# Two attention and two gated-ReLU layers on one core: x loaded by block, layernorm statistics of two blocks on VectorE, q and k projected in fours, logit sums and first output projection placed later

## The chip, the cores and the metric

The kernel runs on one core of one Trainium2 chip. The metric is the device time of one launch in microseconds. The engines are TensorE (PE in the profile; its weight loads are PEld), VectorE (DVE), ScalarE (ACT), GpSimd (POOL) and SyncE (SP), which here only issues DMAs. Each engine works through its own instructions in program order, and an instruction that waits holds up what stands behind it on its engine.

## What is computed

Four residual layers over x of 2048 rows and 1024 columns in bfloat16, an attention layer (A) and a gated layer (B), twice, with the same weights:

```python
x = x + A(layernorm(x)); x = x + B(layernorm(x))
x = x + A(layernorm(x)); x = x + B(layernorm(x))

def A(x):                                   # H = 32 heads of 32, W = 8, dil = 2
    q, k, v = heads(x @ wqkv)
    idx = pos[:, None] - 2 * arange(8)      # each row sees itself and 7 rows before it
    logits = where(idx >= 0, einsum("bhsd,bhswd->bhsw", q, k[idx]) / sqrt(32), -1e9)
    return rows(einsum("bhsw,bhswd->bhsd", softmax(logits), v[idx])) @ wo

def B(x):                                   # F = 3584
    gate = x @ W_gate
    return (gate * (gate > 0) * (x @ W_up)) @ W_down
```

## The kernel before

**Tiling.** x stays on the chip as 16 tiles of 128 rows; 4 tiles make a block of 512 rows, and there are 4 blocks (0 to 3) and 4 layers (L = 0 to 3). Every product is made of chunks of 8 matmuls 128x512 that add up in one of 8 PSUM banks. For a block and an attention layer there are 24 chunks of q, k and v (`plan_proj`, L375), the attention on VectorE (`plan_attn`), and 8 chunks of wo (`plan_wo`, L681), whose results VectorE adds to x (L688). A gated layer has 56 chunks for gate and up (L711) and 56 chunks' worth for down (L757).

**The order of work is written by a planner.** `Plan` keeps a planned clock. `on_pe` places a piece of TensorE work right behind the last one, at 0.216 us per matmul; `at(t, f)` places f at planned time t; `on_dve` and `chain` fill VectorE's planned time: the chain is the attention work in order, each piece with a planned duration and a planned time before which it may not start, and the `on_dve` pieces are put in wherever their time has come. At the end all pieces are sorted by planned time and their instructions are issued in that order, each to its own engine. So planned times set only the order on each engine; the real times come from the waits.

**The start (L = 0, block 0).** `First` normalizes block 0 tile by tile, with transposes on TensorE (L334), between the first chunks of v. SP issues, in this order, x tile 0, v's first weights and x tiles 1 to 3, then q's weights in two halves of 1 MB, k's in two halves (L825), the four tiles of block 1's x (L809), and v's second weights (a slab, L202). Then TensorE does q and k of block 0: two chunks of each, then one of q and one of k in turn, and v's second half.

**The logits of block 0** are made in another way than those of all later blocks (`first_logits`). ScalarE copies each q and k chunk out of PSUM (L449, L452). For each chunk c VectorE multiplies q with the 8 shifted k (`mul`, L471, one instruction) and adds that to a float32 sum in two halves (`add`, L481, from c = 1 on, not for the last c). ScalarE then copies the sum to bfloat16 (`split`, L490), VectorE subtracts the copy and the rest is copied again (`rest`, L503), so that three bfloat16 terms, together with the product of the last chunk, stand for the whole sum. TensorE adds them over the partitions with a matrix of ones (`red`, L512, 32 matmuls). `step` puts `red` behind chunk ("v", 0, 1) of the next block's projection. Then come the softmax (`soft_a` L575 to L581, `expo` L584, `soft_b` L589 to L594), the products with v (`pv_mul` L602, `pv_add` L610 to L613) in 8 groups, the stores to `o_d`, and the loads of `oT` (L621) that wo of block 0 needs. That wo stands behind chunk ("k", 0, 1) of block 3's projection (`wo_hook`).

**Layernorm of the later blocks (`plan_ln`).** For each tile ScalarE makes the sum and the sum of squares (`stats`, L225 and L226); for each pair of tiles VectorE does a few operations on 128x2 numbers (`small_a`), GpSimd raises to the power -0.5 (L239, `pow`), VectorE makes the bias (`small_b`, L244), ScalarE normalizes both tiles (`norm`, L250), and SP transposes the pair by DMA into xnT (`turn`, L256). `late_ln(L, b, t, lag)` places this at planned time t, with `lag` ahead of the transposes. For block b + 1 of layer 0 it is placed 9 us after the start of block b's projection.

**Buffers that matter here.** There is one `xn_all` for all layernorms. `term_1` and `term_2` lie in the buffers of k and q (`hm_pool`), so the loads of the next block's q and k (L537) wait until `red` has read them. `ring` holds 5 slabs of weights of 1 MB; k's weights of layer 0 take two of them.

Of the kernel before, what the change touches and what calls it, by code (L numbers as in the profile page):

```python
# [9 lines left out]
BF16 = mybir.dt.bfloat16  # L10
F32 = mybir.dt.float32
ALU = mybir.AluOpType
ACT = mybir.ActivationFunctionType

P = 128
D = 1024
# [5 lines left out]
KC = D // P  # L22
BLK = 512
TPB = BLK // P
EPS = 1e-5
# [19 lines left out]
def _dram(t, off, dims):  # L45
    return bass.AP(tensor=t.tensor, offset=t.offset + off, ap=[list(d) for d in dims])
# [77 lines left out]
def kernel(  # L124
# [11 lines left out]
    nc = tc.nc  # L136
# [3 lines left out]
    NB = S // BLK  # L140
    NT = S // P
# [3 lines left out]
    x_dram = A_x.flatten_outer_dims()  # L145
# [8 lines left out]
    xpool = ctx.enter_context(tc.tile_pool(name="xres", bufs=1))  # L154
    dram = ctx.enter_context(tc.tile_pool(name="dram", bufs=1, space=bass.MemoryType.DRAM))
    wring = ctx.enter_context(tc.tile_pool(name="wring", bufs=1))
    tpose = ctx.enter_context(tc.tile_pool(name="tpose", bufs=4))
    ln_pool = ctx.enter_context(tc.tile_pool(name="ln", bufs=1))
    stat_pool = ctx.enter_context(tc.tile_pool(name="stat", bufs=2))
# [7 lines left out]
    neg_half = const.tile([P, TPB], F32, name="neg_half")  # L167
# [5 lines left out]
    k_d = [dram.tile([D, ROW], BF16, name=f"k_d{b}") for b in range(NB)]  # L173
    v_d = [dram.tile([D, ROW], BF16, name=f"v_d{b}") for b in range(NB)]
    o_d = [dram.tile([TPB, H, DH, P], BF16, name=f"o_d{b}") for b in range(NB)]
    x_tiles = [xpool.tile([P, D], BF16, name=f"x{t}") for t in range(NT)]

    def consts_early():
        nc.gpsimd.memset(ident[:], 1.0)
# [27 lines left out]
    plan = Plan(RING)  # L207
# [1 line left out]
    w0 = {}  # L209


    def plan_ln(L, b, lag=0.5):
        hold = {}
        clock = [0.0]

        def stats(t):
            def f():
                if t == 0:
                    hold["xn"] = ln_pool.tile([P, TPB, D], BF16, tag="xn_all", name="xn_all")
                    hold["T"] = tpose.tile([P, TPB, KC, P], BF16, tag="T", name=f"xnT_{L}_{b}")  # L220
                if t % 2 == 0:
                    hold[("st", t // 2)] = stat_pool.tile([P, 2, 2], F32, tag="st", name=f"st_{L}_{b}")
                st, xt = hold[("st", t // 2)], x_tiles[b * TPB + t]
                junk = hold["xn"][:, t, :]
                nc.scalar.activation(junk, xt[:], ACT.Identity, accum_out=st[:, 0, t % 2:t % 2 + 1])  # L225
                nc.scalar.activation(junk, xt[:], ACT.Square, accum_out=st[:, 1, t % 2:t % 2 + 1])  # L226
            return f

        def small_a(p):
            st = hold[("st", p)]  # L230
            mean = stat_pool.tile([P, 2], F32, tag="mean", name="mean")
            nc.vector.tensor_scalar(mean[:], st[:, 0, :], 1.0 / D, None, op0=ALU.mult)
            nvar = stat_pool.tile([P, 2], F32, tag="nvar", name="nvar")
            nc.vector.tensor_tensor(nvar[:], st[:, 0, :], mean[:], op=ALU.mult)
            nc.vector.tensor_tensor(nvar[:], nvar[:], st[:, 1, :], op=ALU.subtract)
            vpe = stat_pool.tile([P, 2], F32, tag="vpe", name="vpe")
            nc.vector.tensor_scalar(vpe[:], nvar[:], -1.0 / D, EPS, op0=ALU.mult, op1=ALU.add)  # L237
            rstd = stat_pool.tile([P, 2], F32, tag="rstd", name="rstd")
            nc.gpsimd.tensor_tensor(rstd[:], vpe[:], neg_half[:, 0:2], op=ALU.pow)  # L239
            hold[("mean", p)], hold[("rstd", p)] = mean, rstd  # L240

        def small_b(p):
            nb = stat_pool.tile([P, 2], F32, tag="nb", name="nb")
            nc.vector.scalar_tensor_tensor(nb[:], hold[("mean", p)][:], -1.0, hold[("rstd", p)][:], op0=ALU.mult, op1=ALU.mult)  # L244
            hold[("nb", p)] = nb

        def norm(t):
            def f():
                i, rstd, nb = t % 2, hold[("rstd", t // 2)], hold[("nb", t // 2)]
                nc.scalar.activation(hold["xn"][:, t, :], x_tiles[b * TPB + t][:], ACT.Identity,  # L250
                                     scale=rstd[:, i:i + 1], bias=nb[:, i:i + 1])
            return f

        def turn(t):
            def f():
                nc.sync.dma_start_transpose(hold["T"][:, t - 1:t + 1].rearrange("p t k n -> p (t k) n"),  # L256
                                            hold["xn"][:, t - 1:t + 1].rearrange("p t d -> p (t d)"))
                if t == TPB - 1:
                    xnT[(L, b)] = hold["T"]
            return f  # L260

        def row_done(t):
            def f(now):
                e = max(clock[0], now + 0.3)
                plan.at(e, stats(t))
                clock[0] = e + 2.6
                if t % 2 == 1:
                    plan.on_dve(clock[0], 0.7, lambda: small_a(t // 2), lambda n: after_a(n, t))
            return f

        def after_a(now, t):
            plan.on_dve(now + 1.3, 0.2, lambda: small_b(t // 2), lambda n: after_b(n, t))

        def after_b(now, t):
            e = max(clock[0], now + 0.2)
            plan.at(e, norm(t - 1))
            plan.at(e + 1.25, norm(t))
            clock[0] = e + 2.5
            plan.at(clock[0] + lag, turn(t))

        return [row_done(t) for t in range(TPB)]


    class First:
# [12 lines left out]
        def bn(self, t, h):  # L297
            if h == 0:
                self.st[t] = stat_pool.tile([P, 2, 6], F32, tag="bst", name="bst")
            nc.vector.bn_stats(self.st[t][:, h, :], x_tiles[t][:, 512 * h:512 * h + 512])  # L300
# [38 lines left out]
        def begin(self):  # L339
            self.warm(42)  # L340
            self.bn(0, 0), self.bn(0, 1), self.small(0)
            self.norm(0), self.turn(0), self.warm(4)
            self.copy(0, 0)
            self.bn(1, 0), self.bn(1, 1), self.small(1)
            self.copy(0, 1)
            xnT[(0, 0)] = self.T
            self.norm(1), self.bn(2, 0), self.bn(2, 1)
# [12 lines left out]
    def plan_proj(L, b, hooks={}):  # L360
        ends = {}
        hold = {}
# [36 lines left out]
        steps = [(nm, g, j) for nm, g in (("q", 0), ("k", 0), ("q", 1), ("k", 1), ("v", 0), ("v", 1)) for j in range(4)]  # L399
        if first:  # L400

            fst = First()
            plan.at(-1.0, fst.begin)
            w = w0[("v", 0)]
            for t in range(TPB - 1):
                for h, j in ((h, j) for h in range(2) for j in range(4)):
                    plan.on_pe(1, mms("v", 0, j, w, t, t + 1, KC // 2 * h, KC // 2 * (h + 1)), [w])
                    if h == 1 and j == 2:  # L410
                        e = plan.on_pe(2, lambda t=t: fst.turn(t + 1))
                        plan.at(e, lambda t=t: fst.copies(t + 1))
            steps = [("v", 0, j) for j in range(4)] + [("q", 0, 0), ("q", 0, 1), ("k", 0, 0), ("k", 0, 1)]
            steps += [(nm, c // 4, c % 4) for c in range(2, KC) for nm in "qk"] + [("v", 1, j) for j in range(4)]
        for nm, g, j in steps:
            if L == 0:
                w = w0[(nm, g)]
# [3 lines left out]
            if first and (nm, g) == ("v", 0):  # L421
                e = plan.on_pe(2, mms(nm, g, j, w, TPB - 1, TPB), [w])
            else:
                e = plan.on_pe(8, mms(nm, g, j, w), [w])
# [12 lines left out]
    def first_logits(st, tm):  # L437
        hold = {}
# [84 lines left out]
            plan.at(e + T_EV, out)  # L523
            tm["logits_in"] = e + T_EV + 1.5

        return {"evict": evict}, {("v", 0, 1): step}


    def plan_attn(L, b, ends, st, tm):
# [257 lines left out]
    attn = {}  # L787
    glu = {}
    later_hooks = []
    wo_hook = {("k", 0, 1): lambda: wo(0, 0)}  # L790

    def proj(L, b):
        st, tm = {}, {}
        if L == 0 and b == 0:
            hooks, later_hooks[:] = (lambda h: (h[0], [h[1]]))(first_logits(st, tm))
        else:
            hooks = later_hooks.pop() if later_hooks else wo_hook if L == 0 and b == NB - 1 else {}
        attn[(L, b)] = plan_attn(L, b, plan_proj(L, b, hooks), st, tm)

    def wo(L, b):  # L800
        plan_wo(L, b, attn[(L, b)], plan_ln(L + 1, b))

    def late_ln(L, b, t, lag=0.5):
        for i, f in enumerate(plan_ln(L, b, lag)):
            f(t + 2.7 * i)


    def load_x(t, eng=nc.sync):
        return lambda: eng.dma_start(x_tiles[t][:], x_dram[t * P:(t + 1) * P, :])  # L809
# [20 lines left out]
    w0[("v", 1)] = slab(wqkv_v[:, :, 2 * D + SLAB:3 * D], "wv_0_1", -3.0)  # L830
    for t, at in ((1, -6.7), (2, -6.3), (3, -6.2)):
        plan.at(at, load_x(t))
    plan.at(9.0, consts_late)
    for b in range(1, NB):
        for t in range(b * TPB, (b + 1) * TPB):
            plan.at(-4.5 if b == 1 else 41.5 * (b - 1) + 1.0 * (t % TPB), load_x(t))

    for b in range(NB):
        if b + 1 < NB:
            late_ln(0, b + 1, plan.pe + 9.0, 0.5 if b == 0 else 8.0)  # L840
        proj(0, b)
    for b in range(NB):
        if b >= 1:
# [53 lines left out]
```

## Time and profile before

| | |
|---|---|
| median of 3 runs | 1630.63 us (1629.82 to 1632.91) |
| profiled execution | 1630.63 us, its span 1628.8 us |
| mean granted TensorE clock | 0.998 |
| chain that ended last | PE 94%, DVE 2%, DMA 1%, ACT 1%, issue 1% |
| `L711` gate and up | 3584 matmuls, 379 ns each |
| VectorE and ScalarE over the span | 65% and 29% busy |

The page gives the busy time of each engine, then the chain of work that ended last, followed back from the last instruction, and then groups of equal instructions with their duration and with the idle time of their engine before them. Matmuls overlap: one takes 379 ns, but the next starts 216 ns after it, so a run of them is best measured from start to start. A row of the timeline has the start, the length, the engine, the line, the operation with the tile it writes and those it reads, the shapes, how many like instructions were merged, and in square brackets how long the engine was idle before and what ended that.

### The profile page before, as it was taken

The page shows a single profiled execution, that of the slowest core. Times are in us where ns is not written, and L with a number is a line of the kernel's source. Part 1 is how long each engine was busy: PE and PEld are TensorE (multiplying, and loading weights), DVE is VectorE, ACT ScalarE, POOL GpSimd, SP SyncE. Part 2 cuts the span into 40 slices and gives each one's busy share as a digit, 9 for nine tenths or more (in the row PEclk, how much of TensorE's full clock was granted, in tenths as well). Part 3 has the DMA queues.
Part 4 walks back from the last instruction along what each step waited for, and adds up shares of the span by engine and source line. Part 5 has one row for each costly group of instructions (what it writes and reads, how often), then busy time and mean ns, then how long its engine had stood idle before and what let it go on. Part 6 is the DMA issues. An engine that isn't in the chain of part 4 may idle for free.

```text
span 1628.8 us, 19258 instructions
## 1 busy us (share of the span) xinstructions
PE 1615.7 (99%) x7658; PEld 746.9 (46%) x7658; DVE 1051.0 (65%) x1272; ACT 466.6 (29%) x739; POOL 114.8 (7%) x172
## 2 busy tenths in 40 slices
PE   9989999999999999999999999999999999999999
PEld 7434444444444444444444444444444444444444
DVE  4979989989999259880599716996989211211211
ACT  5665511304230341303413151133021301221110
POOL 3212000001000100011000110000000000000000
PEclk9999999999999999999999999999999999999999
DMA  7678678777956979568886699599846655565442
GB/s 235 166 181 171 187 184 216 195 205 200 237 163 194 257 191 232 160 212 231 198 215 184 199 238 208 160 279 240 220 150 198 197 169 162 175 176 161 156 163 70
DMA packets 443883, 314.83 MB, mean 193 GB/s; under 512 B 195696, under 2 KB 437776, under 8 KB 443792
## 3 DMA queue, kind: packets, MB, share of 16 engines
q1 hardware_dynamic: 414624, 281.39, 64.8%
q10 hardware_dynamic: 24368, 23.40, 4.5%
q0 software_dynamic: 4800, 8.80, 1.6%
q8 instruction: 60, 0.98, 0.3%
q14 instruction: 31, 0.25, 0.1%
HBM read 261.77 MB, written 36.05 MB: 183 GB/s over the span
## 4 chain that ended last, share of the span: by engine, by line
PE 94%; DVE 2%; DMA 1%; ACT 1%; issue 1%; SPq 0%; POOL 0%; ACTq 0%; DVEq 0%
PE acc_u L711 24%; PE acc_g L711 24%; PE dacc L757 24%; PE acc_wo L681 7%; PE acc_v L375 5%; PE acc_q L375 5%; PE acc_k L375 5%; DVE lacc L481 1%; DMA x<-in_A_x_dram 1%; DVE prod L471 1%; DMA xnT<-xn_all 0%; SPq L825 0%; POOL rstd L239 0%; ACT xn_all L225 0%; ACT term L490 0%
## 5 line engine op out<-in xcount | busy, mean ns | idle before, releaser
L711 PEld LDWEIGHTS <-ring 128*128 128x128 bf16 x3584 | 350.7, 98 | 422.9
L711 PE MATMUL acc_g<-xnT,ring 128*128 128x512 bf16 x1792 | 423.3, 379 | 0.0
L711 PE MATMUL acc_u<-xnT,ring 128*128 128x512 bf16 x1792 | 423.3, 379 | 0.0
L757 PE MATMUL dacc<-ring,hT 128*128 128x512 bf16 (+1 forms) x1820 | 388.1, 376 | 0.0
L726 DVE TENSOR_TENSOR hT<-acc_u,r 128x512 bf16<-128x512 f32 x224 | 154.2, 689 | 324.2 <-PE acc_u L711 318.1
L718 ACT ACTIVATE r<-acc_g 128x512 bf16<-128x512 f32 x224 | 133.6, 596 | 709.9 <-PE acc_g L711 709.9
L757 PEld LDWEIGHTS <-hT 128*128 128x128 bf16 x1820 | 178.1, 98 | 209.0
L375 PEld LDWEIGHTS <-ring 128*128 128x128 bf16 x1152 | 115.6, 100 | 133.0
L602 DVE TENSOR_TENSOR pvt<-a,vhm 128x4096 bf16<-128x4096 bf16 x64 | 146.2, 2284 | 0.2
L561 DVE TENSOR_TENSOR l<-l,pr 128x1024 f32<-128x1024 f32 x112 | 136.7, 1221 | 2.2
L551 DVE TENSOR_TENSOR pr<-qhm,khm 128x4096 bf16<-128x4096 bf16 x56 | 127.8, 2282 | 14.2 <-DMA khm<-k_d 14.2
L765 DVE TENSOR_TENSOR x<-dacc,x 128x512 bf16<-128x512 f32 (+1 forms) x65 | 42.8, 679 | 125.4 <-PE dacc L757 125.2
L375 PE MATMUL acc_k<-xnT,ring 128*128 128x512 bf16 x512 | 114.1, 379 | 0.0
L681 PE MATMUL acc_wo<-ring,oT 128*128 128x512 bf16 x512 | 111.8, 379 | 0.0
L375 PE MATMUL acc_v<-xnT,ring 128*128 128x512 bf16 x384 | 84.2, 379 | 0.0
L225 ACT ACTIVATE xn_all<-x 128x1024 bf16<-128x1024 bf16 x60 | 63.3, 1054 | 68.0 <-DVE x L688 62.7
L613 POOL DMA_DIRECT2D o_d<-ohm x64 | 35.4, 553 | 619.9 <-DVE ohm L612 602.8
L610 DVE TENSOR_TENSOR pvt<-pvt 128x2048 bf16<-128x2048 bf16 x64 | 78.1, 1220 | 1.2
L250 ACT ACTIVATE xn_all<-x,nb,rstd 128x1024 bf16<-128x1024 bf16 x60 | 72.2, 1234 | 19.9 <-DVE nb L244 16.3
L681 PEld LDWEIGHTS <-oT 128*128 128x128 bf16 x512 | 50.2, 98 | 60.4
L384 ACT CAST stage_q<-acc_q 128x512 bf16<-128x512 f32 x56 | 32.5, 582 | 157.8 <-PE acc_q L375 154.4
L239 POOL TENSOR_TENSOR rstd<-vpe,neg_half 128x2 f32<-128x2 f32 x30 | 37.0, 1235 | 552.9 <-DVE vpe L237 400.8
(80 smaller groups left out, 839.1 us busy)
## 6 DMA issues: line engine op xcount, KB each, us to landing
ring<-in_B_W_gate_dram SPq DMA_DIRECT2D x56, 1024.0 KB, 7.4
ring<-in_B_W_up_dram SPq DMA_DIRECT2D x56, 1024.0 KB, 5.5
ring<-in_B_W_down_dram SPq DMA_DIRECT2D x48, 1024.0 KB, 6.0
ring<-in_A_wqkv_dram SPq DMA_DIRECT2D x27, 1024.0 KB, 5.6
ring<-in_A_wo_dram SPq DMA_DIRECT2D x16, 1024.0 KB, 7.3
vhm<-v_d SPq DMA_DIRECT2D x32, 284.0 KB, 7.4
v_d<-stage_v ACTq DMA_DIRECT2D x32, 256.0 KB, 6.4
o_d<-ohm POOLq DMA_DIRECT2D x64, 128.0 KB, 4.1
```

Of the source, the lines that this page charges most:

```text
L225: nc.scalar.activation(junk, xt[:], ACT.Identity, accum_out=st[:, 0, t % 2:t % 2 + 1])
L250: nc.scalar.activation(hold["xn"][:, t, :], x_tiles[b * TPB + t][:], ACT.Identity, scale=rstd[:, i:i + 1], bias=nb[:, i:i + 1])
L375: nc.tensor.matmul(acc[:, t0 * P:t1 * P], lhsT=lhsT, rhs=xnT[(L, b)][:, t0:t1, kc, :], start=(kc == 0), stop=(kc == KC - 1))
L551: nc.vector.tensor_tensor(pr[:], st["q"][:], _ap(st["k"], HALO - DIL * w, [[HALO + P, DH], [1, P]]), op=ALU.mult)
L561: nc.vector.tensor_tensor(l[:], pr[:, 0:8] if i == 0 else l[:], pr[:, 8 * i + 8:8 * i + 16], op=ALU.add)
L602: nc.vector.tensor_tensor(tt[:], a_bc, v_sh, op=ALU.mult)
L610: nc.vector.tensor_tensor(tt[:, 0:4], tt[:, 0:4], tt[:, 4:8], op=ALU.add)
L681: nc.tensor.matmul(acc[:], lhsT=st["oT"][:, c, t, :], rhs=ws[half]["t"][:, c, :], start=(c == 0), stop=(c == KC - 1))
L711: nc.tensor.matmul(acc[:], lhsT=w["t"][:, kc, (j % 4) * P:(j % 4 + 1) * P], rhs=xnT[(L, b)][:, :, kc, :], start=(kc == 0), stop=(kc == KC ...
L718: nc.scalar.activation(r[:], hold.pop(("g", j))[:], ACT.Relu)
L726: nc.vector.tensor_tensor(st["hT"][:, j, :], hold.pop(("u", j))[:], hold.pop(("r", j))[:], op=ALU.mult)
L757: nc.tensor.matmul(accs[(t, c0)][:], lhsT=st["hT"][:, j, t * P:(t + 1) * P], rhs=w["t"][:, jl, c0 - half * SLAB:c0 - half * SLAB + n], sta ...
```

## The change

- Blocks 1 to 3 of x become one tile of four (`x_blk`). Block 1 is loaded by one DMA ahead of k's weights, block 2 by one DMA behind v's second slab, block 3 by two at planned time 45; before, each tile had its own load, block 1's behind k's weights, the others at planned times 41.5 and 83 and after.
- For blocks 1 and 3 VectorE takes the statistics (`bn_stats`, two for each tile, and `bn_aggr`) in place of ScalarE; block 2 stays on ScalarE. The three layernorms are placed at 9, 37 and 75.5, the norms of block 3 not before 87, and the transposes' lag is 0.5 for all.
- Block 0's projection goes in fours: v, q, k, q, k, v.
- `red` stands behind ("v", 1, 0) and wo of block 0 behind ("k", 0, 2).
- The constants of GpSimd (`consts_late`) are placed at 22 in place of 9.

```diff
+    x_blk = [xpool.tile([P, TPB, D], BF16, name=f"xb{b}") if b else None for b in range(NB)]
+    x_tiles = [x_blk[t // TPB][:, t % TPB, :] if t >= TPB else xpool.tile([P, D], BF16, name=f"x{t}") for t in range(NT)]
-    x_tiles = [xpool.tile([P, D], BF16, name=f"x{t}") for t in range(NT)]
...
-    def plan_ln(L, b, lag=0.5):
+    def plan_ln(L, b, lag=0.5, on_vector=False, norm_at=0.0):
...
+        def bn(t):
+            def f():
+                if t == 0:
+                    begin()
+                if t % 2 == 0:
+                    hold[("bn", t // 2)] = stat_pool.tile([P, 2, 2, 6], F32, tag="bst2", name="bst2")
+                for h in range(2):
+                    nc.vector.bn_stats(hold[("bn", t // 2)][:, t % 2, h, :], x_tiles[b * TPB + t][:, 512 * h:512 * h + 512])
+            return f
...
         def small_a(p):
+            if on_vector:
+                mv = stat_pool.tile([P, 2, 2], F32, tag="mv2", name="mv2")
+                for i in range(2):
+                    nc.vector.bn_aggr(mv[:, i, :], hold[("bn", p)][:, i].rearrange("p a b -> p (a b)"))
+                nc.vector.tensor_scalar(vpe[:], mv[:, :, 1], EPS, None, op0=ALU.add)
+                nc.gpsimd.tensor_tensor(rstd[:], vpe[:], neg_half[:, 0:2], op=ALU.pow)
+                hold[("mean", p)], hold[("rstd", p)] = mv[:, :, 0], rstd
+                return
...
                 e = max(clock[0], now + 0.3)
-                plan.at(e, stats(t))
-                clock[0] = e + 2.6
+                if on_vector:
+                    plan.on_dve(e, 1.4, bn(t))
+                    clock[0] = e + 1.4
+                else:
+                    plan.at(e, stats(t))
+                    clock[0] = e + 2.6
...
-            e = max(clock[0], now + 0.2)
+            e = max(clock[0], now + 0.2, norm_at)
             plan.at(e, norm(t - 1))
...
-            steps = [("v", 0, j) for j in range(4)] + [("q", 0, 0), ("q", 0, 1), ("k", 0, 0), ("k", 0, 1)]
-            steps += [(nm, c // 4, c % 4) for c in range(2, KC) for nm in "qk"] + [("v", 1, j) for j in range(4)]
+            steps = [(nm, g, j) for nm, g in (("v", 0), ("q", 0), ("k", 0), ("q", 1), ("k", 1), ("v", 1)) for j in range(4)]
...
-        return {"evict": evict}, {("v", 0, 1): step}
+        return {"evict": evict}, {("v", 1, 0): step}
...
-    wo_hook = {("k", 0, 1): lambda: wo(0, 0)}
+    wo_hook = {("k", 0, 2): lambda: wo(0, 0)}
...
-    plan.at(9.0, consts_late)
-    for b in range(1, NB):
-        for t in range(b * TPB, (b + 1) * TPB):
-            plan.at(-4.5 if b == 1 else 41.5 * (b - 1) + 1.0 * (t % TPB), load_x(t))
+    plan.at(22.0, consts_late)
+    for b, n, at in ((1, 4, -5.7), (2, 4, -2.5), (3, 2, 45.0)):
+        for i in range(0, TPB, n):
+            plan.at(at, lambda b=b, n=n, i=i: nc.sync.dma_start(
+                x_blk[b][:, i:i + n, :], _dram(x_dram, (b * BLK + i * P) * D, [[D, P], [P * D, n], [1, D]])))
 
     for b in range(NB):
-        if b + 1 < NB:
-            late_ln(0, b + 1, plan.pe + 9.0, 0.5 if b == 0 else 8.0)
+        if b == 0:
+            late_ln(0, 1, 9.0, on_vector=True)
+            late_ln(0, 2, 37.0)
+            late_ln(0, 3, 75.5, on_vector=True, norm_at=87.0)
         proj(0, b)
```

More of the change, by code (lines that the diff above doesn't have):

```diff
@@ L209, with begin @@
     w0 = {}
-    def plan_ln(L, b, lag=0.5):
+    def plan_ln(L, b, lag=0.5, on_vector=False, norm_at=0.0):
         hold = {}
         clock = [0.0]
+        def begin():
+            hold["xn"] = ln_pool.tile([P, TPB, D], BF16, tag="xn_all", name="xn_all")
+            hold["T"] = tpose.tile([P, TPB, KC, P], BF16, tag="T", name=f"xnT_{L}_{b}")
+        def bn(t):
[7 more added lines that the diff above has]
+            return f
         def stats(t):
@@ L218, in f @@
                 if t == 0:
-                    hold["xn"] = ln_pool.tile([P, TPB, D], BF16, tag="xn_all", name="xn_all")
-                    hold["T"] = tpose.tile([P, TPB, KC, P], BF16, tag="T", name=f"xnT_{L}_{b}")
+                    begin()
                 if t % 2 == 0:
@@ L229, in small_a @@
         def small_a(p):
+            rstd = stat_pool.tile([P, 2], F32, tag="rstd", name="rstd")
+            vpe = stat_pool.tile([P, 2], F32, tag="vpe", name="vpe")
+            if on_vector:
[6 more added lines that the diff above has]
+                return
             st = hold[("st", p)]
@@ L235, in small_a @@
             nc.vector.tensor_tensor(nvar[:], nvar[:], st[:, 1, :], op=ALU.subtract)
-            vpe = stat_pool.tile([P, 2], F32, tag="vpe", name="vpe")
             nc.vector.tensor_scalar(vpe[:], nvar[:], -1.0 / D, EPS, op0=ALU.mult, op1=ALU.add)
-            rstd = stat_pool.tile([P, 2], F32, tag="rstd", name="rstd")
             nc.gpsimd.tensor_tensor(rstd[:], vpe[:], neg_half[:, 0:2], op=ALU.pow)
-            hold[("mean", p)], hold[("rstd", p)] = mean, rstd
+            hold[("mean", p)], hold[("rstd", p)] = mean[:], rstd
         def small_b(p):
             nb = stat_pool.tile([P, 2], F32, tag="nb", name="nb")
-            nc.vector.scalar_tensor_tensor(nb[:], hold[("mean", p)][:], -1.0, hold[("rstd", p)][:], op0=ALU.mult, op1=ALU.mult)
+            nc.vector.scalar_tensor_tensor(nb[:], hold[("mean", p)], -1.0, hold[("rstd", p)][:], op0=ALU.mult, op1=ALU.mult)
             hold[("nb", p)] = nb
@@ L801, in wo, with late_ln @@
         plan_wo(L, b, attn[(L, b)], plan_ln(L + 1, b))
-    def late_ln(L, b, t, lag=0.5):
-        for i, f in enumerate(plan_ln(L, b, lag)):
-            f(t + 2.7 * i)
+    def late_ln(L, b, t, lag=0.5, on_vector=False, norm_at=0.0):
+        for i, f in enumerate(plan_ln(L, b, lag, on_vector, norm_at)):
+            f(t + 2.7 * i * (not on_vector))
     def load_x(t, eng=nc.sync):
```

## The prediction

> **What bounds the kernel now.** I read the page first, then TensorE's waits, its timeline over the first 200 us, VectorE's timeline there, and the landings of the first loads.
>
> ```profile
> PE 1615.7 (99%) x7658; PEld 746.9 (46%) x7658; DVE 1051.0 (65%) x1272; ACT 466.6 (29%) x739; POOL 114.8 (7%) x172
> ```
>
> TensorE (PE) is busy 99%: only what makes it wait can be won. Its waits, longest first, are all in the first 150 us: 4.9 us for the copies of the logit terms (L490), 1.4 at its first instruction, 1.3 for the last term (L503), 1.2 for xnT, and three below 0.5. In its timeline (start, length, engine, line, idle time before and its releaser):
>
> ```profile
> 80.09 3.62 PE L375 MATMUL acc_v<-xnT,wqv 128*128 128x512 bf16 x16
> 83.64 0.61 PE L512 MATMUL L<-prod,wide 128*32 128x512 bf16 x8
> 84.08 0.60 PE L512 MATMUL L<-term,wide 128*32 128x512 bf16 x8
> 84.95 0.40 PE L512 MATMUL L<-term,wide 128*32 128x512 bf16 x4 [0.26 <-ACT term L490]
> 90.03 1.04 PE L512 MATMUL L<-term,wide 128*32 128x512 bf16 x8 [4.68 <-ACT term L490]
> 92.36 0.62 PE L512 MATMUL L<-term,wide 128*32 128x512 bf16 x4 [1.28 <-DVE term L503]
> 92.92 5.07 PE L375 MATMUL acc_v<-xnT,wqv 128*128 128x512 bf16 x16
> 97.82 7.07 PE L375 MATMUL acc_v<-xnT,ring 128*128 128x512 bf16 x32
> 139.26 7.07 PE L375 MATMUL acc_v<-xnT,ring 128*128 128x512 bf16 x32
> 147.51 7.07 PE L375 MATMUL acc_q<-xnT,wqv 128*128 128x512 bf16 x32 [1.18 <-DMA xnT<-xn_all]
> ```
>
> See three losses. The 32 logit sums (L512) need 4 x 0.44 = 1.76 us when nothing waits (8 of them from 83.64 to 84.08) but fill 83.55 to 92.92: **7.61 us**. The 16 matmuls behind them take 4.90 to the next start, where 16 elsewhere take 3.45 (half of 6.91): **1.45**, at a slow array clock. Block 3's xnT comes late: 147.51 - 139.26 - 6.91 = **1.34**. What feeds the sums is VectorE's chain:
>
> ```profile
> 28.08 2.29 DVE L471 TENSOR_TENSOR prod<-q_fm,k_fm 128x4096 bf16<-128x4096 bf16 x1 [12.15 <-ACT k_fm L452]
> 53.32 2.28 DVE L471 TENSOR_TENSOR prod<-q_fm,k_fm 128x4096 bf16<-128x4096 bf16 x1
> 60.05 2.28 DVE L471 TENSOR_TENSOR prod<-q_fm,k_fm 128x4096 bf16<-128x4096 bf16 x1
> 84.93 2.29 DVE L503 TENSOR_TENSOR term<-lacc,term 128x2048 bf16<-128x2048 f32 x1 [1.52 <-ACT term L490]
> 90.02 2.29 DVE L503 TENSOR_TENSOR term<-lacc,term 128x2048 bf16<-128x2048 f32 x1 [2.79 <-ACT term L490]
> ```
>
> It idles 12 us before its first product, because ScalarE sits on block 1's late x (waits: 2.6 us, L225) and evicts k's chunk 0 at 27.41, though TensorE had it at 23.1. Then it runs 6.73 us per chunk and ends at 92.31, with small layernorm operations between and two waits for ScalarE, which has block 2's norms ahead of the term copies.
>
> **The change, part by part.** One chunk (8 matmuls) is 1.727 us. The planner's clock and the trace run together from q's start (planned 8.21, seen 17.93): I add 9.7.
>
> *Loads.* Block 1's x, 1 MB in one issue, goes ahead of k's. Landings from issue:
>
> ```profile
> L825 SPq DMA_DIRECT2D ring<-in_A_wqkv_dram x1: 2745/2745/2745, 6.6 to 6.6; - x1
> DMA to landing us min/median/max: 14.6/14.6/14.6
> L809 SPq DMA_DIRECT2D x<-in_A_x_dram x1: 1147/1147/1147, 13.1 to 13.1; - x1
> DMA to landing us min/median/max: 12.2/12.2/12.2
> ```
>
> k's second half lands at 6.63 + 14.6 = 21.2, the last of block 1's x at 25.3; q's second half landed at 15.8 (4.73 + 11.1), k's first at 18.5 (5.29 + 13.2). So x1 now lands at about 15.8 + 2.7 = 18.5, and k's second half between 23.9 (2.7 us per MB) and 25.3 (same bytes by then as before). With q in fours, k is first wanted at 17.93 + 4 x 1.727 = 24.84, its second half at 25.7. Taken: no wait, margin 0.4; far bound below. Block 2's x issues right behind v's second slab, block 3's after wo's; both are wanted tens of us later. SP has three issues fewer; its next work, block 1's transposes, waits for the norms anyway.
>
> *Statistics of block 1.* Eight bn_stats at 0.65 (a pair takes 1.29) = 5.2 us, two small_a of 0.6, two small_b: 7.3 us from 18.5, done by 25.8, inside VectorE's 12 us of idle. Without that cover the chain starts up to 5.2 later. ScalarE loses 8 x 1.15 = 9.4 us there. It does norm(0), then evicts k0 (TensorE 26.57, plus 0.2) by 27.4: the first product stays near 27.4 (28.08 now), the second follows k1 and two norms at 30.25.
>
> *The chain then.* Chunks at 6.73 put product 4 at 50.4. Block 2's statistics, planned at 37, put their small operations around it: 4 x 0.16 plus 0.75 for POOL's pow, twice, 2.8. Product 7 is at 73.4, the four L503 at 2.25 follow, end **84.8** against 92.31. ScalarE must keep up: from 46.3 to the first term copy (planned 61.4, so 71.1) it has 14 evictions (8.2), 7 store issues (3.2), stats 9.4, norms 4.8: 25.6 in 24.8, so 1 us late at most, by which VectorE may slip 1 or 2.
>
> *Sums later.* After ("v",1,0) instead of ("v",0,1): three chunks, 5.2 us. TensorE is there at 83.55 + 5.18 = 88.73, 4 us after the last term. The 7.61 and the 1.45 go.
>
> *What waits behind.* SP's first load of block 1's q (L537) needs term_2's buffer, so it now waits for sums that end near 90.5 (92.98 now); behind it stand block 3's transposes, ready near 100 only, then khm. No loss.
>
> *Block 3.* Its bn_stats and small_a (6.5 us) fill VectorE from 84.8 to 91.4, before soft_a, which waits for the sums anyway (90.5 plus 1.1 of copies: 91.6; now 94.06). Without that gap soft_a is 6.5 late. Transposes run near 100 to 110, xnT is wanted at 137: the 1.34 goes. Small operations (4.4 us) leave block 0's pv groups.
>
> *wo of block 0, one chunk later*, is reached at 90.5 + 3 + 24 + 7 chunks = 149.2. soft_a 91.6, exp behind one eviction, soft_b (3.8) to 99.6, eight pv groups of 4.66 to 137, then, as now (145.67 to 149.30, landing 3.3 after), oT at 143.9: margin 5.3, now 157.87 - 152.6 = 5.3. Without the later hook it would be 3.6. Later blocks keep their distances to TensorE, within 1 us.
>
> *Constants (L184)* go behind POOL's pows; zpad is wanted at 59.6, wide at 88. Nothing.
>
> **Sum:** 7.61 + 1.45 + 1.34 = 10.4; 1628.8 - 10.4 = 1618.4. The execution took 1630.63, the median, so 1.83 lies around the span: **1620.2**.
>
> **Rivals.**
> A. *The chain is not earlier* (ScalarE's backlog or pow eats the 7.5 us). It ends at 92.3, the sums at 92.98 instead of 90.5: 2.5 us stay, **1622.7**. For: 25.6 us of ScalarE work in 24.8. Against: its two waits today came from norms that now run 15 us earlier. The Trainium skill, "TensorE: Matmul & The Clock Gate", Part 1, has the array at half clock after an idle window of about 3.4 us; the 4.68 us idle here agrees, and by it this shorter wait costs no slow stretch, while without it 1.45 comes on top (1624.2).
> B. *k's weights come last.* If they land at 30.4, as v's slab did (14.30 + 16.1) beside the first v_d stores, TensorE waits 4.7: **1624.9**. Against: the slab had another MB and zpad's small packets beside it.
> C. *ScalarE takes the place of VectorE*: term copies late by as much as the sums moved. The 9.06 stays, 1.34 goes: **1629.3**. It would need 9 us of lag, I find 1 or 2.
> D. *Slower: the shared x tile.* Four x tiles of blocks 1 to 3 become one. If waits were kept per tile, each wo addition (L688) would wait for ScalarE's statistics of its neighbour: a stage is 4 x (1.29 + 2.33) + 2.48 of norms = 17.0 against 13.8, 3.15 in each of six stages, 18.9: **1639.1**; from 1.7 a stage on it is a loss. Against: SP loads a slab of ring at 170.15 while wo's matmuls read another part of it; norm(2) writes xn_all at 39.97 while the transposes of its first half, issued 36.93, are under way.
>
> **Numbers.** Forecast 0.73, A 0.11, B 0.05, C 0.05, D 0.06. 0.2% is 3.3 us, what a measurement here can tell. Below 1627.4 lie forecast, A and B: 0.89; C is the same, 0.05; D slower, 0.06. The median runs spread -0.8 to +2.3 us. The forecast's own range is 1619 to 1623; with A and half of B it is 1618.5 to 1625.
>
> **What would show it.** TensorE's list of waits without L512 or xnT; L512's 32 sums within 2 us; the matmuls behind at 3.45 per 16; VectorE's last L503 ending at 84 to 88 and bn_stats in its two gaps; k's first matmul at 24.84 without a wait; wo of block 0 near 149 without one. A wait at the first acc_k shows B, one at acc_wo a late oT, L688 idle for ScalarE shows D. I am wrong if TensorE waits again after 25 us.

## The result, and the profile after

The changed kernel takes 1621.2 us (median of 6 runs, 1620.36 to 1622.18) against 1630.62 us: a ratio of 0.9941, 95% interval 0.9928 to 0.9954. It is faster by 9.4 us, 0.6%. The profiled execution took 1621.7 us, its span is 1620.0 us, 8.8 less than before.

The page's first line, TensorE still at 99%:

```profile
PE 1609.8 (99%) x7609; PEld 745.5 (46%) x7658; DVE 1060.6 (65%) x1284; ACT 450.5 (28%) x707; POOL 111.1 (7%) x172
```

VectorE has 9.6 us more to do and ScalarE 16 less. TensorE's list of waits is now complete in five rows (engine, line, what it waited for, us in total, times, longest):

```profile
PE warm L321 <- POOL neg_half L183: 1.4, 1, 1.4
PE acc_v L401 <- DMA wqv<-in_A_wqkv_dram: 0.9, 1, 0.9
PE tp L360 <- DVE xn_all L355: 0.8, 1, 0.8
PE acc_k L401 <- DMA ring<-in_A_wqkv_dram: 0.6, 1, 0.6
PE acc_v L401 <- ACT xnT L363: 0.5, 2, 0.2
```

Neither the logit sums nor xnT are in it. New is the 0.6 us at the first k matmuls. The same places in TensorE's timeline (line numbers have moved by some 25):

```profile
18.51 7.08 PE L401 MATMUL acc_q<-xnT,wqv 128*128 128x512 bf16 x32
25.43 1.03 PE L401 MATMUL acc_k<-xnT,ring 128*128 128x512 bf16 x4
27.01 6.26 PE L401 MATMUL acc_k<-xnT,ring 128*128 128x512 bf16 x28 [0.56 <-DMA ring<-in_A_wqkv_dram]
...
88.37 1.89 PE L401 MATMUL acc_v<-xnT,ring 128*128 128x512 bf16 x8
90.19 0.61 PE L537 MATMUL L<-prod,wide 128*32 128x512 bf16 x8
90.63 1.47 PE L537 MATMUL L<-term,wide 128*32 128x512 bf16 x24
92.03 5.35 PE L401 MATMUL acc_v<-xnT,ring 128*128 128x512 bf16 x24
97.22 7.07 PE L401 MATMUL acc_q<-xnT,wqv 128*128 128x512 bf16 x32
```

The sums take 92.03 - 88.37 - 1.73 (one chunk) = 1.93 us where they took 9.37, and the 24 matmuls behind them take 5.19, full speed. From 138.66 on block 3's q follows without a gap, and wo of block 0 begins at 150.75 without one. VectorE's chain, and what it does in the gap behind it:

```profile
78.34 4.49 DVE L528 TENSOR_TENSOR lacc<-lacc,term 128x2048 f32<-128x2048 f32 x2
82.74 4.54 DVE L528 TENSOR_TENSOR term<-lacc,term 128x2048 bf16<-128x2048 f32 x2
87.20 2.46 DVE L228 BATCH_NORM_STATS2 bst<-xb 128x6 f32<-128x512 bf16 x4
```

The last term is done at 87.28, with no wait for ScalarE, and block 3's statistics follow at once.

### The profile page after: what moved, and what is told of

The parts are those of the page before. It is cut to its first block, busy times and chain, and to the rows that moved or that the text cites. A ratio compares the mean times of both kernels' runs of the same rounds, so it can differ in the third digit from the quotient of the medians.

```text
span 1620.0 us, 19174 instructions
## 1 busy us (share of the span) xinstructions
PE 1609.8 (99%) x7609; PEld 745.5 (46%) x7658; DVE 1060.6 (65%) x1284; ACT 450.5 (28%) x707; POOL 111.1 (7%) x172
## 4 chain that ended last, share of the span: by engine, by line
PE 98%; DMA 1%; SPq 1%; issue 0%; DVE 0%; DVEq 0%
PE acc_u L736 24%; PE acc_g L736 24%; PE dacc L782 24%; PE acc_k L401 7%; PE acc_wo L706 7%; PE acc_v L401 6%; PE acc_q L401 6%; DMA ring<-in_A_wqkv_dram 1%; SPq L850 0%; PE L L537 0%; SPq L834 0%; SPq L861 0%; DVE xb L790 0%; SPq L854 0%; SPq L838 0%
## 5 line engine op out<-in xcount | busy, mean ns | idle before, releaser
L790 DVE TENSOR_TENSOR xb<-dacc,xb 128x512 bf16<-128x512 f32 (+1 forms) x49 | 32.6, 678 | 120.4 <-PE dacc L782 120.0
L586 DVE TENSOR_TENSOR l<-pr 128x1024 f32<-128x1024 bf16 x56 | 68.2, 1218 | 0.6
L593 DVE TENSOR_TENSOR l<-l 128x512 f32<-128x512 f32 x112 | 62.3, 556 | 3.0
L261 POOL TENSOR_TENSOR rstd<-vpe,neg_half 128x2 f32<-128x2 f32 x26 | 26.7, 1026 | 540.8 <-DVE vpe L260 540.6
```

The costliest lines, as they stand in the source:

```text
L586: nc.vector.tensor_tensor(l[:], pr[:, 0:8] if i == 0 else l[:], pr[:, 8 * i + 8:8 * i + 16], op=ALU.add)
L593: nc.vector.tensor_tensor(l[:, 0:n], l[:, 0:n], l[:, n:2 * n], op=ALU.add)
```

## The experiments

Every kernel was timed beside the kernel before, at least five runs each, on one chip for each group of four; the ratios are to the kernel before on the same chip. The first moves the sums without the rest of the change, the next six undo one part each, the eighth splits a load. "Loss at the sums" is the time between the chunks on either side of the logit sums (L512, or L537 and L538 where lines have moved) less 1.76 us for the sums, as in the prediction. A "slow stretch" is the run of TensorE matmuls behind a wait that takes longer than its full pace of 0.216 us each.

### The sums alone moved

In the kernel before:

```diff
-        return {"evict": evict}, {("v", 0, 1): step}
+        return {"evict": evict}, {("v", 1, 0): step}
-    wo_hook = {("k", 0, 1): lambda: wo(0, 0)}
+    wo_hook = {("q", 1, 1): lambda: wo(0, 0)}
```

> The kernel before with the logit sums behind ("v", 1, 0) and wo of block 0 behind ("k", 0, 3); loads, statistics and the order of q and k as before. My theory: moving the sums alone takes most of their stall away, because VectorE's chain still ends at 92.3 while TensorE now reaches the sums at 88.7, so 2.5 us of 9.06 stay; but block 3's transposes hang on VectorE and ScalarE, which do not move, so xnT still lands near 147, and what is won comes back there as a longer wait (1.3 grows to about 7): 1629 us. Rival, every loss is won by itself: 1624.0 us, with the wait for xnT still near 1.3.

The kernel that ran differs from this text in one place: wo of block 0 stands behind ("q", 1, 1), four chunks later than in the kernel before, and not behind ("k", 0, 3), which would be two.

Measured: 1638.56 us, ratio 1.005 (1.0038 to 1.0063): **slower than before**. Both theories missed, mine in the place and the size. TensorE's timeline of that kernel:

```profile
92.60 5.35 PE L375 MATMUL acc_v<-xnT,ring 128*128 128x512 bf16 x24
103.31 9.18 PE L375 MATMUL acc_q<-xnT,wqv 128*128 128x512 bf16 x32 [5.36 <-DMA xnT<-xn_all]
112.33 7.07 PE L375 MATMUL acc_k<-xnT,ring 128*128 128x512 bf16 x32
...
207.71 3.57 PE L711 MATMUL acc_g<-xnT,ring 128*128 128x512 bf16 x8 [4.38 <-DMA xnT<-xn_all]
```

SP's queue in the same stretch:

```profile
92.71 0.54 SPq L537 DMA_DIRECT2D qhm<-q_d  x1
93.29 4.16 SPq L256 DMA_TRANSPOSE xnT<-xn_all  x1
```

and in the kernel before:

```profile
93.02 0.54 SPq L537 DMA_DIRECT2D qhm<-q_d  x1
93.61 3.90 SPq L256 DMA_TRANSPOSE xnT<-xn_all  x1
```

The loss at the sums fell from 7.61 to 2.08 and the slow stretch behind them (1.45) went, nearly as expected. But block **2**, not 3, now comes late: the second half of its transposes stands on SP behind the load of q (L537), which waits until the sums have read term_2's buffer. Its norms are done at 88.1, and it is issued at 93.29, where TensorE wants its result at 97.8. The kernel before has the same order and nearly the same times, but there TensorE, held up at the sums, wants the result only at 104.73: the stall at the sums hid this wait. It costs 5.53 (103.31 - 92.60 - 5.18), 2.11 of slow matmuls behind it, and 1.04 go at block 3. Gate and up also wait for their xnT, 4.54 and 2.79 of slow matmuls: wo of block 0 begins at 165.18 in place of 157.87, and the last transposes that hang on it are issued at 192.75, behind two 1 MB loads, and land 14.8 us later. In all 18.1 where the kernel before loses 10.4. Without these 7.3 it would be 10.8, so by the trace the sums alone win nothing, and that this kernel is slower comes from wo's place. A kernel with the sums moved and wo less far was not run.

### The changed kernel with one part undone

**Sums back.** `{("v", 1, 0): step}` becomes `{("v", 0, 1): step}`.

> The changed kernel with the logit sums back behind ("v", 0, 1). My theory: the chain itself is 5 us earlier, so TensorE, there at 84.9, waits for a last term that ends at 87.3: a loss of 1.1 us, an idle time too short for a slow stretch behind it, 1622.3 us. Rival, the later place is what removed the stall: 5 us or more stay and the slow stretch comes back, 1626 us or more.

Measured: 1621.51 us, 0.9945 (0.9932 to 0.9959), the same as the changed kernel. One wait of 0.63 us at the sums (loss 1.00), no slow stretch: as my theory has it. Once the chain is early, the later place of the sums adds nothing that can be timed.

**x behind k.** Block 1's load at -5.2 in place of -5.7.

> The changed kernel with block 1's x loaded behind k's weights instead of ahead. My theory: TensorE's 0.6 us wait at the first acc_k goes, k's second half landing near 24.3, but x lands near 27, the statistics end near 33.6, the first product starts some 5 us later, the chain ends near 92 and TensorE waits 1.5 to 2 us at the sums: 1622.2 us. Rival, only k's lateness counts: 1620.5 us, no wait at the sums.

Measured: 1620.67 us, 0.9935 (0.9923 to 0.9948); the rival's number. x landed at 25.4, not 27, the first product started at 32.52, 3.8 us later and not 5, and the chain ended at 89.88, not 92; the other half of the difference is that block 2's small operations waited less for pow (0.61 and 0.59 where the changed kernel waited 1.80 and 0.59). With the sums at 89.30 that is just in time, loss 0.18. So x ahead of k is not needed either, though without it there is no margin left: the last term is ready 0.6 us after the sums begin.

**q and k in turn.** The two lines of `steps` of the kernel before.

> The changed kernel with q and k of block 0 in turn as before. My theory: the fours are there for k's weights: k's second half is then wanted at 22.8 and lands at 27.0, so TensorE waits about 4.1 us instead of 0.6 and all behind it moves: 1624.6 us, or 1626 if a slow stretch follows that wait. Rival, the fours are there for VectorE's chain (wait at the sums) and k's place is harmless: 1621 us with no wait at acc_k beyond 1 us.

Measured: 1626.68 us, 0.9970 (0.9958 to 0.9981), the second of my numbers. The wait is at the place named, with a slow stretch behind it (12 matmuls in 4.34 us, 1.75 too many):

```profile
21.09 1.07 PE L401 MATMUL acc_k<-xnT,ring 128*128 128x512 bf16 x4
26.74 4.50 PE L401 MATMUL acc_k<-xnT,ring 128*128 128x512 bf16 x12 [4.58 <-DMA ring<-in_A_wqkv_dram]
31.08 1.89 PE L401 MATMUL acc_q<-xnT,wqv 128*128 128x512 bf16 x8
```

**Block 1's statistics on ScalarE.** `late_ln(0, 1, 9.0)`.

> The changed kernel with block 1's statistics on ScalarE as before (x still loaded ahead of k). My theory: 9.4 us of statistics on ScalarE between 19 and 31 hold up the copy of k's chunk 0, the first product starts near 31.7 instead of 28.75, 2.8 us of small operations go into the chain, which ends near 93: TensorE waits about 2 us at the sums, 1623.3 us. Rival, VectorE's statistics of block 1 buy nothing, the early x and the later sums are enough: 1621.2 us, no wait at the sums.

Measured: 1620.76 us, 0.9935 (0.9922 to 0.9947); the rival's number. The first product started at 29.30, not 31.7, and the chain ended at 88.19, not 93: a loss of 0.17 at the sums. I had laid all four tiles' statistics, 9.4 us, ahead of k's first copy; in the trace three of them stand ahead of it (it starts at 28.68) and the fourth behind it.

**wo of block 0 back.** `("k", 0, 1)`, and `t + 4.0` for `t + 5.0` in `after_pv`.

> The changed kernel with wo of block 0 back behind ("k", 0, 1), two instead of three k chunks ahead of it being done; the planned time of oT's loads is put 1 us earlier, so that they still stand ahead of it in the order. My theory: oT lands at 144.9 and wo would begin at 149.0, margin 4: no wait, 1621.2 us. Rival, wo's later place is needed to hide oT: a wait at acc_wo of 1 us or more and 1622.5 us or more.

Measured: 1621.13 us, 0.9938 (0.9924 to 0.9952), no wait at acc_wo: my theory. With oT's loads planned 1 us earlier, wo's later place is not needed.

**Block 3's statistics on ScalarE.** `late_ln(0, 3, 75.5, norm_at=87.0)`.

> The changed kernel with block 3's statistics on ScalarE as before, at the same planned times. My theory: VectorE's gap before soft_a is free, so what stands in it costs and saves nothing; ScalarE's 9.4 us delay the copies of the sums and with them soft_a by a few us, which the 5.8 us ahead of wo of block 0 take up: 1621.2 us, no wait at acc_wo or xnT. Rival, VectorE's statistics of block 3 are needed: oT or xnT comes late, TensorE waits 1 us or more.

Measured: 1620.63 us, 0.9935 (0.9922 to 0.9947): my theory. TensorE's only wait past the start is 1.3 us for k's weights. The price is paid in margin: oT's first load is issued at 146.05 and lands 3.1 later, 1.8 us ahead of wo where the changed kernel has 5.8.

**x in two halves around k.**

```diff
-    for b, n, at in ((1, 4, -5.7), (2, 4, -2.5), (3, 2, 45.0)):
+    for b, n, at in ((1, 2, -5.7), (2, 4, -2.5), (3, 2, 45.0)):
...
-            plan.at(at, lambda b=b, n=n, i=i: nc.sync.dma_start(
+            plan.at(at + 0.5 * (b == 1 and i > 0), lambda b=b, n=n, i=i: nc.sync.dma_start(
```

> The changed kernel with block 1's x in two loads of two tiles, one ahead of k's weights and one behind them. My theory: k's second half lands 1.3 us earlier, at 25.6 against a need at 26.3, so the 0.6 us wait goes; VectorE's statistics of the second pair end some 2 us later, the chain ends near 89.5, still before the sums need it: 1620.5 us. Rival, the chain loses more than that and TensorE waits at the sums: 1621.5 us or more.

Measured: 1620.6 us, 0.9933 (0.9921 to 0.9946). The wait for k is gone and the sums wait for nothing, as my theory has it; the chain ends at 86.9, earlier than the 89.5 it gave. But 0.6 us less than the changed kernel is inside the spread of the runs. It is a version as good as the changed one; that it beats it is not shown.

### What carries the gain

Five of the undone parts cost nothing that can be timed, so the gain has to hang on what they share: the layernorms' places, or any one of several parts that stand in for each other. Four kernels more.

**Only the places.** The changed kernel with all of the above undone: only the layernorms of blocks 2 and 3 stay at 37 and 75.5, with the early loads.

In the changed kernel:

```diff
-            late_ln(0, 1, 9.0, on_vector=True)
+            late_ln(0, 1, 9.0)
             late_ln(0, 2, 37.0)
-            late_ln(0, 3, 75.5, on_vector=True, norm_at=87.0)
+            late_ln(0, 3, 75.5, norm_at=87.0)
```

Besides, x of block 1 at -5.2, q and k in turn, the sums behind ("v", 0, 1), wo behind ("k", 0, 1) and `consts_late` at 9.0.

> Of the change only the earlier places of the layernorms of blocks 2 and 3 and the earlier loads of their x: statistics all on ScalarE, block 1's x behind k, q and k in turn, the sums behind ("v", 0, 1), wo of block 0 behind ("k", 0, 1), GpSimd's constants at 9. My theory: with block 2's norms gone from ScalarE's queue ahead of the term copies the chain ends near 88, so some 3.3 us of the 9.06 at the sums stay, without a slow stretch, and the 1.34 at xnT goes: 1623.5 us. Rival, the sums' later place or VectorE's statistics carry the gain: the stall at the sums stays above 6 us, 1627 us or more.

Measured: 1629.01 us, 0.9981 (0.9972 to 0.9990). The 1.34 at block 3's xnT went, as my theory says; the sums did not follow it (a loss of 7.40, and 1.42 behind them), and the number is the rival's:

```profile
84.56 0.62 PE L538 MATMUL L<-term,wide 128*32 128x512 bf16 x8
87.28 0.40 PE L538 MATMUL L<-term,wide 128*32 128x512 bf16 x4 [2.11 <-ACT term L516]
90.11 1.04 PE L538 MATMUL L<-term,wide 128*32 128x512 bf16 x8 [2.42 <-ACT term L516]
92.43 0.62 PE L538 MATMUL L<-term,wide 128*32 128x512 bf16 x4 [1.29 <-DVE term L529]
92.99 5.03 PE L401 MATMUL acc_v<-xnT,wqv 128*128 128x512 bf16 x16
```

The norms no longer hold up the term copies (block 2's last norm ends at 75.3, the first term copy waits for the chain until 78.60). But x of block 1 is now one load and lands as a whole: ScalarE takes its first tile at 25.90, where it took it at 21.98, and the first product starts at 31.99 where it started at 28.08. The chain ends at 92.38, as before. So this kernel also carries a cost of the single load; the early places with block 1's x in four loads were not run.

**Block 2's place back.** `late_ln(0, 2, 51.8, 8.0)` in the changed kernel.

> The changed kernel with block 2's layernorm placed as before (51.8, its transposes 8 us behind the norms). My theory: its second transposes stand behind the load of q on SP that waits for the sums, as in the run with the sums alone moved, so xnT of block 2 comes about 5 us after TensorE wants it at 97, a slow stretch of 2 us follows, and ScalarE's term copies come behind the norms again: 1628 us, with the longest wait at acc_q for xnT. Rival, VectorE's chain alone decides: 1622 us, a wait at the sums and none for xnT.

Measured: 1628.91 us, 0.9992 (0.9983 to 1.0001): the gain is gone, all but at most 0.2%. The loss at the sums is 2.48, xnT of block 2 costs 4.43, the slow matmuls behind it 1.47:

```profile
93.33 5.35 PE L401 MATMUL acc_v<-xnT,ring 128*128 128x512 bf16 x24
102.94 8.54 PE L401 MATMUL acc_q<-xnT,wqv 128*128 128x512 bf16 x32 [4.25 <-DMA xnT<-xn_all]
111.32 7.07 PE L401 MATMUL acc_k<-xnT,ring 128*128 128x512 bf16 x32
```

SP's queue there, and the same transposes in the changed kernel, where q's first load is issued at 92.14, behind them:

```profile
93.44 0.54 SPq L562 DMA_DIRECT2D qhm<-q_d  x1
94.03 4.49 SPq L278 DMA_TRANSPOSE xnT<-xn_all  x1
```

```profile
69.48 3.72 SPq L278 DMA_TRANSPOSE xnT<-xn_all  x1
```

Block 2's norms are done at 88.8, but its second transposes are issued at 94.03, right behind q's first load: SP's queue, as with the sums alone. VectorE waits for ScalarE's term copies again, 4.46 and 2.25, and that is the loss at the sums. A kernel that changes SP's order alone was not run; that the 5.9 us at xnT come from it is read from these rows.

**Block 3's place back.** `late_ln(0, 3, 95.3, 8.0)` and wo behind `("k", 0, 3)`.

> The changed kernel with block 3's layernorm placed as before (95.3, on ScalarE, its transposes 8 us behind the norms), and wo of block 0 behind ("k", 0, 3), where its loads still stand ahead of it. My theory: xnT of block 3 lands near 145, where TensorE wants it at 138.7: a wait of about 6 us with a slow stretch of 1.5 to 2 behind it, 1628 to 1629 us. Rival, with the sums' stall gone all that feeds the transposes comes earlier too, and the wait stays near the 1.3 of before: 1622.5 us.

Measured: 1621.96 us, 0.9952 (0.9938 to 0.9967); the rival's number. xnT lands at 138.58, not 145, and TensorE waits 1.10: with the sums' stall gone, all that feeds these transposes comes earlier too (they are issued from 127.98 on, from 136.95 in the kernel before).

**q and k in turn, x behind k.** Both parts undone together.

> The changed kernel with q and k of block 0 in turn and block 1's x behind k's weights. My theory: the fours are needed only because x goes ahead of k; with both undone the 4.6 us wait at acc_k of the run with q and k in turn is gone, the first product starts near 32 to 33, and the sums wait 0 to 1 us: 1621 us. Rival, q and k in turn cost by themselves: 1624 us or more.

Measured: 1621.25 us, 0.9939 (0.9926 to 0.9951): my theory, with 1.2 us of wait at the sums. So the fours buy nothing that can be timed but room for x ahead of k, and x ahead of k is not needed.

## Why the prediction was right, point by point

- **The three losses** (10.4 us). The sums' 7.61 came to 7.44, because the 32 sums take 1.93 us in place, not 1.76; the slow stretch (1.45) and block 3's xnT (1.34) went entirely. That they are what the kernel had to win holds.
- **k's weights: the term that was mis-sized.** "Taken: no wait, margin 0.4." k's second half landed at 27.0 (issued at 10.0, 17.0 later), not at 25.3, and cost 0.72 us. This is the prediction's own sign of being wrong, a wait of TensorE after 25 us, and the only one. It was to come in at the latest when the same bytes had come in before; the landing was later than that. The price changes from run to run: TensorE's list has none in the kernel with the sums back and 1.3 with block 3 on ScalarE, where the loads stand in the same order and k's second half landed at 25.6 and 27.2. The first half of rival B is thus true, at a seventh of its price.
- **The start.** q of block 0 begins 0.58 us later (18.51 for 17.93). TensorE waited 0.9 us for the second half of v's first weights, which the change does not touch; they landed at about 9.1 (2.74 + 6.4), and at about 8.5 (2.74 + 5.8) before. Kernels whose start is the same as the changed one's begin q at 18.00 (sums back) and 18.72 (wo back), so the runs scatter here by as much. With 0.17, 0.72 and 0.58 off, 10.4 becomes 8.9; the spans differ by 8.8. The median's 9.4 is larger, as the six spans run from 1618.7 to 1620.5 and the profiled one is among the slow half.
- **The chain.** Forecast to end at 84.8 with a slip of 1 or 2, it ended at 87.28: 1.3 of that is the later start (28.75 for 27.4), 1.2 one longer wait for pow (1.80 for 0.6). That wait is GpSimd's queue and not pow itself, which took 0.72 there: ahead of it stood a store of v, issued at 57.41, that waited for ScalarE's copy. ScalarE was not late for it at all: it waited 1.94 for the chain before its first copy. The forecast of 25.6 us of work in 24.8 was too dark. (In it 8 x 1.15 is 9.2 and not 9.4; the statistics' rows start 1.18 apart, which gives the 9.4.)
- **What waits behind.** SP's load of q waits for the sums (issued at 92.14), block 3's transposes behind it cost nothing, wo of block 0 has its margin (oT at 144.9, wo at 150.75: 5.8 where 5.3 was forecast). The prediction named block 3 behind that load, and not block 2, whose earlier place keeps its transposes out of it. That is a coupling it did not see. With block 2 back in its place nearly all of the gain is gone, and by the trace 5.9 of the 8.4 us lost there are this coupling. The prediction had block 2's early layernorm for ScalarE's sake alone; that it also cleared SP's queue was luck, as far as its working goes.
- **Rivals.** A, C and D did not come. D's place would show as VectorE's additions (L713) waiting for ScalarE; they wait for TensorE alone. On A's sentence about the slow stretch see the last section.

What the prediction took for a sum of parts is, as far as the runs go, a conjunction: block 2's layernorm early, *and* something that keeps TensorE from waiting for the chain, the sums later or the chain earlier. Without block 2's early layernorm the gain is gone, and the early layernorms without the rest win 0.2%. With the early layernorms the sums' place, VectorE's statistics of either block, x's place, wo's place and the fours can each be undone at no cost that can be timed, save that the fours are needed while x goes ahead of k; block 3's place costs a wait of 1.10 us, too little to time. Which single part would do beside the early layernorms, the sums' place or one of those that make the chain earlier, was not tried.

## What to carry to other kernels

Before moving a consumer later to hide its wait, list what else waits for that consumer: here a load that reuses its buffer, and behind that load, on SP, which issued them in program order, another block's transposes. A wait that is removed can uncover the next one, which it hid. When several edits hide the same stall, undo them one at a time from the finished kernel and also apply one alone: the first test finds the spare ones, the second finds the ones that need company. A load that is made larger is waited for as a whole, so its first user can start later: 25.90 in place of 21.98 here, when x of block 1 became one load.

## What the hardware showed that was not expected

The slow stretch does not need one long wait. In the run with only the places moved, no wait of TensorE at the sums is longer than 2.42 us, yet the 16 matmuls behind them took 4.87 to the next start (92.99 to 97.86) instead of 3.45, as in the kernel before with its 4.68. The weight loads there come at a spacing of 0.43 us until 95.91:

```profile
95.09 0.15 PEld L401 LDWEIGHTS <-wqv 128*128 128x128 bf16 x1 [0.28 <-issue]
95.52 0.15 PEld L401 LDWEIGHTS <-wqv 128*128 128x128 bf16 x1 [0.28 <-issue]
95.91 1.61 PEld L401 LDWEIGHTS <-wqv 128*128 128x128 bf16 x8 [0.24 <-issue]
```

In both kernels the granted clock reads 1.00 from 88 to 89, 0.52 from 89 to 90, 0.50 up to 94, 0.53 from 94 to 96 and 1.00 again behind that. In the kernel before TensorE had been idle since 85.4 when the clock fell, 3.7 us. In the run with only the places moved it had been idle from 85.2 to 87.3, had done one row of 0.40 us, and was idle again: the clock fell at the same time without one gap of that length. After a single wait of 1.23 us (q and k in turn, x behind k) or 0.63 us (sums back) with full work on either side, the next chunks ran at full speed; after 4.25, 4.38, 4.58 and 5.36 they did not (1.47, 2.79, 1.75 and 2.11 us lost). The Trainium skill, "TensorE: Matmul & The Clock Gate", Part 1, puts the half clock after an idle window of about 3.4 us. The single waits agree with it, and the split wait does not, if the window is read as one unbroken gap. The same part of the Trainium skill describes a monitor that sets the clock by how busy the array has been recently. By that a thinly filled stretch can count as well, and this run is such a case.
